# A router and two feed-forward layers on one core: token rows gathered in quarters and transposed on VectorE

## The chip, the cores and the metric

The kernel runs on one core of a Trainium2 chip. The metric is the device time of one execution in microseconds (us), the median of three runs. Engines are named as the profile names them: PE is TensorE's matmul, PEld its weight load, DVE is VectorE, ACT is ScalarE, POOL is GpSimd, and SP is SyncE, which issues most transfers.

## The reference

```python
B, H, S, D = 4, 12, 448, 64          # attention; N = B*S = 1792 tokens of H*D = 768
scores = q @ k.T / sqrt(D) - log(S)
attn_out = sigmoid(scores) @ v       # -> x[1792, 768]

logits = x @ w_gate                  # 8 experts, each takes cap = 224 tokens:
# the pairs (token, expert) are walked in falling order of logit; a token goes to the
# first expert that still has room
for e in range(8):
    out[mask_e] = relu(x[mask_e] @ w1[e]) @ w2[e]      # 768 -> 1024 -> 768

h = out @ w_in                       # 768 -> 2048
return (s * relu(h)**2 + b) @ w_out  # 2048 -> 768
```

Everything is float32. The kernel keeps that precision by splitting each operand into a high part (`float32r`) and a low part, the remainder, and summing three products: high by high, high by low and low by high.

## The kernel before, in words

The order of the work is written out by hand (`manual_schedule`): each engine executes its instructions in the order in which the program names them, and semaphores are put in where data are shared.

**Attention and routing.** The first part computes attention, writes the token rows to a scratch tensor `xs` in DRAM, and decides by an auction which 224 tokens go to which expert. `places` leaves the token numbers in `idx`, a tile of 128 partitions by 2 halves by 8 experts: column e of half h holds the rows of expert e, 128 in the first half and 96 in the second. `keep_clock` puts matmuls on zeros into PE's queue while PE has nothing else to do. `gather(0)` then fetches the rows of expert 0, and a branch (`go_on`) on a flag skips the fallback of the auction.

**Four groups.** The rest is a loop over g = 0..3. Each group has three stages:

- *Experts*: `expert(2g)` and `expert(2g+1)`, each with 8 weight units of the first layer (`w1`, 6 blocks of 128x128) and 6 of the second (`w2`, 8 blocks). `half_mm` does a unit with two matmuls per block, 448 columns (high and low of the data side by side) and 224 columns; the last two units of `w1` use `short_mm`. After each unit, ACT and DVE make the high and low parts of the result.
- *Hidden*: 16 units (`f` in `range(KG)`), each of 18 matmuls of 448 columns, then square, scale and shift on ACT and DVE.
- *Output*: two halves `h`, 8 units (`span`) each, with three tiles of 128 rows in even groups and four in odd groups, 6 matmuls of 384 columns per tile and unit. The results go to `orow` and are written to the output by `scatter` on POOL's queue, later, in the next even expert.

**Weights.** All units stand in one list. `advance`, called once per unit, issues the load of a unit up to 8 ahead (`w_dma`, on SP), makes the low part of a unit 4 ahead (`w_low`) and the high part of one 5 ahead (`w_high`, on ACT). There are 4 raw buffers and 5 each for high and low, so a load waits until the low part of the unit four places in front has been made. The list `where` says which low parts POOL makes; the others are DVE's:

```python
where += [n in (0, 2, 4, 6, 12) for n in range(KF + KD)]   # L171, for every expert
```

**Rows of an expert.** `gather(e)` issues two indirect DMAs on POOL's queue, 128 and 96 rows of 3 KB. `x_split(e, n)`, n = 0..3, transposes three 128-column blocks of one half on PE (L653) into PSUM; ACT copies the high part to `xg[e]` (L655) and DVE subtracts to make the low part (L656). An even expert's four pieces are put into the hidden stage of the group in front (L778, at f = 3, 7, 11, 15), an odd expert's into the even expert in front of it (L710, at f = 1 to 4). `gather(2g+2)` is issued behind `expert(2g)` (L757), `gather(2g+3)` behind the hidden stage (L782).

**Other work in these stages.** `row_ids` (16 small copies on POOL, L632) makes the lists for `scatter`; it stands behind `gather(1)`, in front of the first expert (L751). In group 0, `late_convert` (four DVE instructions, L151 to L154, each time on a 768 KB load into one buffer) brings the last 8 blocks of 64-bit weights to float32: five times in the hidden stage, three times in the output stage (h = 0, units 0, 2 and 4).

Of the kernel before, what the change touches and what calls it, by code (L numbers as in the profile page):

```python
# [8 lines left out]
F32 = mybir.dt.float32  # L9
F32R = mybir.dt.float32r  # L10
BF16 = mybir.dt.bfloat16
I32 = mybir.dt.int32
# [18 lines left out]
KG = F2 // 128  # L31
HT = (128, CAP - 128)
DH = DM // 2
LEVELS = 8
GROW = 2.0
MARGIN = 0.25
# [20 lines left out]
C_FLAT = C_F + LEVELS + 2  # L57
C_SEL = C_FLAT + CP
C_OFF = C_SEL + E
C_END = C_OFF + LEVELS + 2  # L60


@with_exitstack
def tile_kernel(ctx, tc, qT, kT, v, wg, w1, w2, wi, wo, s2, b2, cst, out):
# [4 lines left out]
    wraw = ctx.enter_context(tc.tile_pool(name="wraw", bufs=4))  # L69
    wsp = ctx.enter_context(tc.tile_pool(name="wsp", bufs=5))  # L70
    wlp = ctx.enter_context(tc.tile_pool(name="wlp", bufs=5))
    xrp = ctx.enter_context(tc.tile_pool(name="xrp", bufs=2))
    dpool = ctx.enter_context(tc.tile_pool(name="dpool", bufs=1, space=DRAM))
    ctx.enter_context(tc.manual_schedule())

# [3 lines left out]
    sb2 = const.tile([128, 2], F32, name="sb2")  # L79
    idx = const.tile([128, 2, E], I32, name="idx")  # L80
    idt = const.tile([128, 3, 4], I32, name="idt")
    idl = const.tile([128, 2], I32, name="idl")
    spacer = const.tile([1, 1], F32, name="spacer")

# [82 lines left out]
    for g in range(4):  # L167
        for e in (2 * g, 2 * g + 1):
            units += [(w1[e, f], KD, True) for f in range(KF)]
            units += [(w2[e, d], KF, True) for d in range(KD)]  # L170
            where += [n in (0, 2, 4, 6, 12) for n in range(KF + KD)]  # L171
        units += [(narrow[i], wide[i][1], False) for i in range(len(wide))]
        where += [False] * len(wide)
    raws, splits = {}, {}
# [188 lines left out]
    for n, c in ((0, C_ID), (2, C_SAMEE), (3, C_PREV), (4, C_TRI), (5, C_NEGE)):  # L363
        G.tensor_copy(cb[:, n], ct[:, c:c + 128])
    V.scalar_tensor_tensor(cb[:, 1], ct[:, C_ID:C_ID + 128], -2.0, ct[:, C_SAMEC:C_SAMEC + 128],
                           op0=ALU.mult, op1=ALU.add)
    G.tensor_copy(off, ct[:2, C_OFF:C_END])
    G.memset(two, 1.0)
    G.tensor_copy(slot, ct[:, C_SLOT:C_SLOT + CAP])
    identb, rival, samee, prev, tri, nege = (cb[:, n] for n in range(6))  # L370
# [145 lines left out]
    oh = rp.tile([CP, NCH, CAP], BF16, name="oh")  # L516
    ia = rp.tile([128, 2, E], F32, name="ia")
    Pf = P.rearrange("p c e -> p (c e)")

    def places(rest=lambda: None):  # L520
        pp = ps_1.tile([CP, 128], F32, name="pa")
        T.matmul(pp, ch, identb, start=True, stop=True)
        V.tensor_copy(cw, cnt0.to_broadcast([128, CP]))
        po = ps_r.tile([CP, NCH, E], F32, name="pi")
        pof = po.rearrange("p c e -> p (c e)")
        T.matmul(pof, cw, prev, start=True, stop=False)
        V.tensor_copy(Pf, pp)
        T.matmul(pof, tri[:CP, :CP], Pf, start=False, stop=True)
        V.tensor_mul(pm_, po, P)
        V.reduce_sum(pos, pm_, axis=AX.X)  # L530
        for c in range(NCH):
            V.tensor_scalar(oh[:, c], slot[:CP], pos[:, c:c + 1], None, op0=ALU.is_equal)
            if c == 2:
                pk = count()
            if c == 5:
                full(pk)
                rest()
            if c == 3:
                G.tensor_mul(R[:, :, 0, :], P, ct[:CP, C_CIDX:C_CIDX + 128].rearrange("p (c e) -> p c e", e=E))
                A.mul(R[:, :, 1, :], P, ct[:CP, C_P:C_P + 1])  # L540
        pis = [ps_r.tile([n, 2, E], F32, name="pi") for n in HT]
        for c in range(NCH):
            for h, n in enumerate(HT):
                T.matmul(pis[h].rearrange("p a e -> p (a e)"), oh[:, c, h * 128:h * 128 + n],
                         R[:, c].rearrange("p a e -> p (a e)"), start=(c == 0), stop=(c == NCH - 1))
        for h, n in enumerate(HT):
            A.copy(ia[:n, h], pis[h][:, 1])
            V.scalar_tensor_tensor(idx[:n, h], pis[h][:, 0], float(CP), ia[:n, h], op0=ALU.mult, op1=ALU.add)

    xr = {}  # L550

    def gather(e):
        if e >= E:
            return
        for h, n in enumerate(HT):
            if (e, h) not in xr:
                xr[e, h] = xrp.tile([128, DM], F32, name="xr")
            G.indirect_dma_start(out=xr[e, h][:n], out_offset=None, in_=xs,
                                 in_offset=bass.IndirectOffsetOnAxis(ap=idx[:n, h, e:e + 1], axis=0))

    auction(STEPS, True)
    places(lambda: rows(len(turns)))
# [42 lines left out]
    def go_on(steps):  # L605
        rv = nc.values_load(flag[0:1, 0:1], min_val=0, max_val=128)
        with tc.If(rv < 128):
            if steps:
                auction(steps[0], False)
                full(count())  # L610
                go_on(steps[1:])
            else:
                greedy()
            if steps == MORE:
                places()
                gather(0)

    gather(0)
    go_on(MORE)
    rt.close()  # L620
    early.close()
# [22 lines left out]
    def x_split(e, n):  # L644
        if e >= E:
            return
        if n == 0:
            xg[e] = m2p.tile([128, KD, 2, CAP], F32R, name="x")
        h, k0 = n // 2, n % 2 * 3
        m = HT[h]  # L650
        px = ps_x.tile([128, 3, 128], F32, name="px") if e else ps_m.tile([128, 3, 128], F32, name="acc")
        for k in range(3):
            T.transpose(px[:, k, :m], xr[e, h][:m, (k0 + k) * 128:(k0 + k + 1) * 128], ident[:m, :m])  # L653
        xh = xg[e][:, k0:k0 + 3, 0, h * 128:h * 128 + m]
        A.copy(xh, px[:, :, :m])  # L655
        V.tensor_sub(xg[e][:, k0:k0 + 3, 1, h * 128:h * 128 + m], px[:, :, :m], xh.bitcast(F32))  # L656
# [38 lines left out]
    def expert(e, y):  # L695
        x = xg.pop(e)
        u = ml.tile([128, KF, 2, CAP], F32R, name="u")
        for f in range(KF):
# [7 lines left out]
                if f == KF - 2:  # L706
                    advance()
            if 1 <= f <= 4:
                if e % 2 == 0:
                    x_split(e + 1, f - 1)  # L710
                if out_rows:
                    scatter(*out_rows.pop(0))
        sl = slice((e % 2) * CAP, (e % 2 + 1) * CAP)
        for d in range(KD):
            wh, wl = w_get()
            half_mm(wh, wl, u, KF, AF.Copy, (y[:, d, 0, sl], y[:, d, 1, sl]), d < KD - 1)

    def scatter(ids, row):
        G.memset(spacer, 0.0)
# [24 lines left out]
        last["i"] += 1  # L744
        late_in()

    stores, out_rows = [], []
    for n in (0, 2, 1, 3):
        x_split(0, n)
    gather(1)  # L750
    row_ids()  # L751
    last["buf"] = ml.tile([128, 3072], I32, name="orow")
    late_in()
    for g in range(4):
# [8 lines left out]
        for f in range(KG):  # L763
# [9 lines left out]
            else:  # L773
                A.activation(gn[:, f, 0], r, AF.Identity, bias=sb2[:, 1:2])  # L774
            V.scalar_tensor_tensor(gn[:, f, 1], r, sb2[:, 1:2], gn[:, f, 0].bitcast(F32),
                                   op0=ALU.add, op1=ALU.subtract)
            if f % 4 == 3:
                x_split(2 * g + 2, f // 4)  # L778
            advance()
            if not g and f % 3 == 1:  # L780
                late_convert()
        gather(2 * g + 3)  # L782
        tiles = [(128 * t, idt[:, t - 1, g:g + 1]) for t in range(1, 4)]
        if g % 2:
            tiles = [(0, idl[:, g // 2:g // 2 + 1])] + tiles
# [2 lines left out]
        for h in range(2):  # L788
# [3 lines left out]
            for span in spans:  # L792
                ws = {u: [w.rearrange("p k c -> p (k c)") for w in w_get()] for u in span}
                for t, (c0, ids) in enumerate(tiles):
# [8 lines left out]
                    if span[-1] == n - 1:  # L803
# [8 lines left out]
                            scatter(ids, orow[:, t])  # L812
                        elif h:
                            out_rows.append((ids, orow[:, t]))
                advance()
                if not g and not h and span in ([0], [2], [4]):
                    late_convert()
# [2 lines left out]
def _consts(np):  # L820
# [17 lines left out]
    c[1, C_OFF] = 0.0  # L838
    c[:2, C_OFF + LEVELS + 2 - SIGNS:C_OFF + LEVELS + 2] = np.float32([[NT - CAP], [0.5]])
    c[:, C_FLAT:C_FLAT + CP] = FLATC - ((CP * ch[:, None] + np.arange(CP)[None]) * E + e[:, None])  # L840
    c[:, C_SEL:C_SEL + E] = (p[:, None] % 32) == np.arange(E)[None]
    return c


def _layout(np, i):
    c = np.ascontiguousarray

    def heads(a):
# [4 lines left out]
        "kT": c(heads(i["k"]).transpose(0, 1, 2, 4, 3).reshape(B, NP, 128, S)),  # L853
        "v": c(i["v"].reshape(B, NP, 2, NC, CP, D).transpose(0, 1, 4, 3, 2, 5).reshape(B, NP, CP, NC, 128)),
        "wg": c(i["moe_w_gate"].reshape(KD, 128, E).transpose(1, 0, 2)),
        "w1": c(i["moe_w1"].reshape(E, KD, 128, KF, 128).transpose(0, 3, 2, 1, 4)),
        "w2": c(i["moe_w2"].reshape(E, KF, 128, KD, 128).transpose(0, 3, 2, 1, 4)),
        "wi": c(i["moe2_w_in"].reshape(KD, 128, KG, 128).transpose(2, 1, 0, 3)).view(np.int64),
        "wo": c(i["moe2_w_out"].reshape(8, 2, 128, 2, DH).transpose(3, 0, 2, 1, 4)
# [22 lines left out]
```

## Time and profile before

| | before |
|---|---|
| three runs | 944.69 us median (944.27 to 946.06) |
| profiled execution | 946.52 us, span 944.7 us |
| PE busy | 917.0 us, 97% of the span |
| PEld, DVE, ACT, POOL busy | 84%, 62%, 48%, 15% |
| mean granted TensorE clock | 0.983 |

The span runs from the first to the last instruction; 1.8 us of the profiled time lie around it. The profiled execution was 1.83 us above the median of the three runs. Busy time is what the engines' records cover; matmuls are pipelined, so that a matmul's own duration is longer than the step from one to the next. "Idle before" in a timeline names what ended the wait.

### The profile page before, as it was taken

To read this page: it belongs to the slowest core of one execution; us is meant where nothing else is said; L and a number is where in the kernel's file an instruction comes from. 1 tells how busy PE (TensorE), PEld (TensorE's weight loads), DVE (VectorE), ACT (ScalarE), POOL (GpSimd) and SP (SyncE) were. 2 spreads that over 40 slices of the span, in tenths; PEclk is the share of its full clock that TensorE was granted. 3 is DMA by queue.
4 is the path that set the end of the run, shared out by engine and by line. 5 is a ranking of instruction groups with operands and counts; after the bars stand their busy time and mean duration, and the time that the engine had idled before them with its cause. 6 is when DMAs were issued, how large, how long until landed. Compare 5 with 4: busy or idle time off the path is not lost.

```text
span 944.7 us, 14521 instructions
## 1 busy us (share of the span) xinstructions
PE 917.0 (97%) x5467; PEld 797.0 (84%) x5467; DVE 587.6 (62%) x1043; ACT 449.3 (48%) x787; POOL 138.1 (15%) x136
## 2 busy tenths in 40 slices
PE   9999999688999999999999999999999999999997
PEld 4454555568999999999999999999999999999997
DVE  3877875645868875578776224786773287777320
ACT  6666767735654432566333225564332366433120
POOL 1000003224410000442000004420000232100001
PEclk9999999779999999999999999999999999999999
DMA  9989993844746666567334235763444476433311
GB/s 307 321 298 341 321 323 111 241 134 167 239 144 214 219 230 217 179 222 230 119 117 141 90 101 165 232 218 122 129 127 137 119 251 211 137 120 108 126 34 68
DMA packets 68459, 173.12 MB, mean 183 GB/s; under 512 B 7968, under 2 KB 24864, under 8 KB 68384
## 3 DMA queue, kind: packets, MB, share of 16 engines
q1 hardware_dynamic: 66112, 161.13, 52.9%
q0 software_dynamic: 2272, 11.01, 3.4%
q8 instruction: 44, 0.72, 0.3%
q14 instruction: 31, 0.25, 0.1%
HBM read 148.52 MB, written 23.59 MB: 182 GB/s over the span
## 4 chain that ended last, share of the span: by engine, by line
PE 56%; DVE 10%; DMA 5%; ACT 3%; issue 2%; POOL 1%; POOLq 0%; SPq 0%; ACTq 0%; DVEq 0%
PE acc L661 9%; PE acc L801 7%; PE acc L802 7%; PE acc L800 7%; PE acc L727 6%; PE acc L728 6%; PE acc L729 6%; PE acc L662 4%; DVE wl L201 4%; DMA raw<-in_w_dram 3%; DMA orow<-in_wo_dram 2%; ACT wh L190 1%; DVE y L675 1%; ACT gt L774 1%; DVE r L770 1%
## 5 line engine op out<-in xcount | busy, mean ns | idle before, releaser
L190 ACT CAST wh<-raw 128x768 fp32r<-128x768 f32 (+1 forms) x240 | 208.8, 877 | 160.6 <-PE acc L802 115.7
L201 DVE TENSOR_TENSOR wl<-raw,wh 128x768 fp32r<-128x768 f32 (+1 forms) x198 | 207.2, 1053 | 91.1 <-ACT wh L190 91.1
L201 POOL TENSOR_TENSOR wl<-raw,wh 128x768 fp32r<-128x768 f32 (+1 forms) x42 | 92.6, 2213 | 414.8 <-ACT wh L190 414.7
L801 PE MATMUL acc<-wl,gt 128*128 128x384 f32 x448 | 150.4, 336 | 1.8 <-DVE wl L201 1.8
L800 PE MATMUL acc<-wh,gt 128*128 128x384 f32 x448 | 150.6, 336 | 0.0
L802 PE MATMUL acc<-wh,gt 128*128 128x384 f32 x448 | 150.4, 336 | 0.0
L727 PE MATMUL acc<-y,wh 128*128 128x448 f32 x384 | 141.4, 368 | 0.0
L729 PE MATMUL acc<-y,wl 128*128 128x448 f32 x384 | 140.6, 366 | 0.0
L728 PE MATMUL acc<-y,wh 128*128 128x448 f32 x384 | 140.6, 366 | 0.0
L661 PE MATMUL acc<-u,wh 128*128 128x448 f32 x384 | 121.9, 376 | 1.8 <-DVE u L685 1.5
L662 PE MATMUL acc<-u,wl 128*128 128x224 f32 x384 | 101.4, 264 | 0.0
L661 PE MATMUL acc<-x,wh 128*128 128x448 f32 x288 | 94.4, 383 | 0.7 <-DVE x L656 0.7
L251 ACT ACTIVATE attn<-psc,nls 112x896 f32<-112x896 f32 x96 | 88.8, 1008 | 9.4 <-PE psc L249 9.4
L769 ACT ACTIVATE r<-acc 128x448 f32<-128x448 f32 x64 | 34.8, 543 | 116.7 <-PE acc L729 116.7
L801 PEld LDWEIGHTS acc<-wl,gt 128*128 128x128 f32 x448 | 84.7, 189 | 2.1 <-DVE wl L201 2.1
L800 PEld LDWEIGHTS acc<-wh,gt 128*128 128x128 f32 x448 | 84.7, 189 | 0.0
L802 PEld LDWEIGHTS acc<-wh,gt 128*128 128x128 f32 x448 | 84.5, 189 | 0.0
L662 PE MATMUL acc<-x,wl 128*128 128x224 f32 x288 | 76.8, 267 | 3.0 <-POOL wl L201 3.0
L661 PEld LDWEIGHTS acc<-u,wh 128*128 128x128 f32 x384 | 72.1, 188 | 8.9 <-DVE u L685 3.6
L260 PE MATMUL pv<-attn,vt 112*64 112x448 f32 x384 | 77.5, 545 | 0.0
L729 PEld LDWEIGHTS acc<-y,wl 128*128 128x128 f32 x384 | 72.1, 188 | 6.3
L728 PEld LDWEIGHTS acc<-y,wh 128*128 128x128 f32 x384 | 72.2, 188 | 6.1
(212 smaller groups left out, 1306.7 us busy)
## 6 DMA issues: line engine op xcount, KB each, us to landing
raw<-nw SPq DMA_DIRECT2D x128, 384.0 KB, 3.0
raw<-in_w_dram SPq DMA_DIRECT2D x64, 384.0 KB, 3.9
raw<-in_w_dram SPq DMA_DIRECT2D x48, 512.0 KB, 4.5
craw<-in_wi_dram SPq DMA_DIRECT2D x16, 768.0 KB, 5.8
nw<-co SPq DMA_DIRECT2D x24, 384.0 KB, 7.7
craw<-in_wo_dram SPq DMA_DIRECT2D x8, 768.0 KB, 6.3
orow<-in_wo_dram SPq DMA_DIRECT2D x8, 768.0 KB
rqk<-in_kT_dram SPq DMA_DIRECT2D x24, 224.0 KB, 6.9
```

Of the source, the lines that this page charges most:

```text
L190: A.copy(h[:, :k], raws[i][:, :k])
L201: eng.tensor_sub(lo[:, :k], r[:, :k], h[:, :k].bitcast(F32))
L251: A.activation(attn[n][:, :, c, :], p[:, :, :S], AF.Sigmoid, bias=nls[:CP], scale=1.0 / math.sqrt(D))
L260: T.matmul(pv[j * 64:(j + 1) * 64, :S], v[:, c, j * D:(j + 1) * D], a[:, j, c, :], start=(c == 0), stop=(c == NC - 1))
L661: T.matmul(p[:, :2 * CAP], wh[:, k], src[:, k].rearrange("p a s -> p (a s)"), start=(k == 0), stop=False)
L662: T.matmul(p[:, :CAP], wl[:, k], src[:, k, 0], start=False, stop=(k == n - 1))
L727: T.matmul(p, wh, src[:, k, 0], start=first, stop=False)
L728: T.matmul(p, wh, src[:, k, 1], start=False, stop=False)
L729: T.matmul(p, wl, src[:, k, 0], start=False, stop=last)
L800: T.matmul(ps[t][:, :DH], hi, wh[:, cols], start=(f == 0), stop=False)
L801: T.matmul(ps[t][:, :DH], hi, wl[:, cols], start=False, stop=False)
L802: T.matmul(ps[t][:, :DH], lo, wh[:, cols], start=False, stop=(f == KG - 1))
```

## The change

From expert 2 on, a gather fetches quarter rows: `xs` is seen as 7168 rows of 192 columns, and each of seven indirect DMAs brings 32 tokens, of each the four quarters to four groups of 32 partitions. With 32 tokens by 192 columns on each group of 32 partitions, a transpose of 32 by 32 blocks on DVE gives the layout that the matmuls need, with the contracted dimension in another order; the rows of `w1` for experts 2 to 7 are put into the same order on the host. `x_split` for these experts moves to the output stage of the group in front (units 1 to 4 of each half), and its subtraction to the unit behind. `gather(2g+3)` follows the even expert's last transpose there. The index list `idq` for the quarters is made by `spread`, behind `gather(0)`, with seven small matmuls. Besides this, `row_ids` moves into expert 0's second layer, and POOL makes the low parts of units 6 and 12 alone for experts 1 to 7.

```diff
-    xrp = ctx.enter_context(tc.tile_pool(name="xrp", bufs=2))
+    xrp = ctx.enter_context(tc.tile_pool(name="xrp", bufs=1))
...
-            where += [n in (0, 2, 4, 6, 12) for n in range(KF + KD)]
+            where += [n in ((0, 2, 4, 6, 12) if e else (6, 12)) for n in range(KF + KD)]
...
@@ places, at c == 3
                 A.mul(R[:, :, 1, :], P, ct[:CP, C_P:C_P + 1])
+                A.copy(pick, ident.rearrange("p (j r) -> p j r", r=32)[:, :, None, :].to_broadcast([128, 4, 4, 32]))
...
+    def spread():
+        for h, n in enumerate(HT):
+            V.tensor_copy(idf[:n, h], idx[:n, h])
+        pq = ps_r.tile([128, NJ, E], F32, name="pi")
+        for j in range(NJ):
+            n = HT[j // 4]
+            T.matmul(pq[:, j], pick[:n, j % 4].rearrange("p q r -> p (q r)"), idf[:n, j // 4], start=True, stop=True)
+        V.tensor_scalar(idq, pq, 4.0, ct[:, C_QUAD:C_QUAD + 1], op0=ALU.mult, op1=ALU.add)
+
     def gather(e):
         if e >= E:
             return
-        for h, n in enumerate(HT):
-            if (e, h) not in xr:
-                xr[e, h] = xrp.tile([128, DM], F32, name="xr")
-            G.indirect_dma_start(out=xr[e, h][:n], out_offset=None, in_=xs,
-                                 in_offset=bass.IndirectOffsetOnAxis(ap=idx[:n, h, e:e + 1], axis=0))
+        if e not in xr:
+            xr[e] = xrp.tile([128, 2 * DM], F32, name="xr")
+        if e < 2:
+            for h, n in enumerate(HT):
+                G.indirect_dma_start(out=xr[e][:n, h * DM:(h + 1) * DM], out_offset=None, in_=xs,
+                                     in_offset=bass.IndirectOffsetOnAxis(ap=idx[:n, h, e:e + 1], axis=0))
+        else:
+            for j in range(NJ):
+                G.indirect_dma_start(out=xr[e][:, j * DQ:(j + 1) * DQ], out_offset=None,
+                                     in_=xs.rearrange("t (q d) -> (t q) d", q=4),
+                                     in_offset=bass.IndirectOffsetOnAxis(ap=idq[:, j, e:e + 1], axis=0))
...
     gather(0)
+    spread()
     go_on(MORE)
...
@@ x_split
+        if e > 1:
+            j0, nj = 2 * n, min(2, NJ - 2 * n)
+            px = ps_x.tile([128, 2 * DQ], F32, name="px")[:, :nj * DQ]
+            V.transpose(px, xr[e][:, j0 * DQ:(j0 + nj) * DQ])
+            px = px.rearrange("p (j k r) -> p k j r", j=nj, r=32)
+            hi, lo = (xg[e][:, :, a, j0 * 32:(j0 + nj) * 32].rearrange("p k (j r) -> p k j r", r=32) for a in range(2))
+            A.copy(hi, px)
+            rest.append((lo, px, hi))
+            return
...
@@ expert
             if 1 <= f <= 4:
-                if e % 2 == 0:
-                    x_split(e + 1, f - 1)
+                if not e:
+                    x_split(1, f - 1)
...
             half_mm(wh, wl, u, KF, AF.Copy, (y[:, d, 0, sl], y[:, d, 1, sl]), d < KD - 1)
+            if not e and d == 1:
+                row_ids()
...
     gather(1)
-    row_ids()
...
@@ hidden stage
-            if f % 4 == 3:
-                x_split(2 * g + 2, f // 4)
             advance()
             if not g and f % 3 == 1:
                 late_convert()
-        gather(2 * g + 3)
...
@@ output stage, after the matmuls of a unit
+                for lo, px, hi in rest:
+                    V.tensor_sub(lo, px, hi.bitcast(F32))
+                rest.clear()
+                if g < 3 and 1 <= span[0] <= 4:
+                    x_split(2 * g + 2 + h, span[0] - 1)
+                    if not h and span[0] == 4:
+                        gather(2 * g + 3)
                 advance()
```

`spread` also stands in the fallback of the auction, behind its `gather(0)`. The constants get one more column, `C_QUAD` (p // 32).

## Rows read from the trace of the kernel before

**Rows 1.** The page, part 1: busy us (share of the span) and instructions.

```profile
PE 917.0 (97%) x5467; PEld 797.0 (84%) x5467; DVE 587.6 (62%) x1043; ACT 449.3 (48%) x787; POOL 138.1 (15%) x136
```

**Rows 2.** Windows by stage: length, PE, PEld, DVE, ACT, POOL busy, clock, DMA, GB/s.

```profile
207.06:243.95 36.89, 33.91 (x217) 31.83 (x217) 23.11 (x37) 20.17 (x42) 16.97 (x24) 0.95 0.55 182
243.95:274.82 30.87, 30.58 (x206) 29.13 (x205) 24.07 (x38) 20.05 (x41) 8.28 (x5) 1.00 0.72 228
...
334.89:388.53 53.64, 51.89 (x291) 51.57 (x290) 28.15 (x37) 16.83 (x23) 4.79 (x3) 0.97 0.64 212
388.53:420.05 31.52, 31.52 (x218) 30.32 (x217) 25.24 (x37) 20.41 (x42) 15.28 (x12) 1.00 0.70 224
...
609.41:641.27 31.86, 30.87 (x206) 29.15 (x205) 24.25 (x38) 20.15 (x41) 8.89 (x5) 1.00 0.70 222
641.27:701.33 60.06, 60.06 (x302) 55.04 (x301) 43.44 (x67) 21.52 (x36) 0.98 (x1) 1.00 0.37 113
701.33:751.34 50.01, 50.01 (x291) 50.01 (x290) 16.82 (x21) 15.07 (x20) 4.59 (x3) 1.00 0.46 140
...
813.67:872.05 58.38, 58.38 (x290) 54.12 (x289) 42.04 (x63) 20.45 (x33) 0.00 (x0) 1.00 0.36 109
```

**Rows 3.** Timeline of POOL in expert 0: start, us, instruction [idle before].

```profile
207.61 0.92 POOL L558 DMA_INDIRECT xr<-xs,idx  x1 [0.30 <-issue]
212.00 3.68 POOL L632 COPY idt<-idx 32x4 int32<-32x4 int32 x12 [3.48 <-DMA xr<-xs,idx]
...
216.64 4.26 POOL L201 TENSOR_TENSOR wl<-raw,wh 128x768 fp32r<-128x768 f32 x2
```

**Rows 4.** Timeline of PE in expert 0, fifth weight unit.

```profile
219.17 0.37 PE L662 MATMUL acc<-x,wl 128*128 128x224 f32 x1 [2.96 <-POOL wl L201]
```

**Rows 5.** Window of four us behind that wait, columns as in group 2.

```profile
219.00:223.00 4.00, 3.83 (x16) 3.60 (x17) 0.00 (x0) 0.30 (x1) 1.90 (x2) 0.59 0.72 240
```

**Rows 6.** Timeline of PE in expert 2, around one group of three transposes.

```profile
392.18 0.27 PE L662 MATMUL acc<-x,wl 128*128 128x224 f32 x1
392.28 0.49 PE L653 MATMUL px<-ident,xr 128*128 128x128 f32 x3
...
392.81 0.26 PE L662 MATMUL acc<-x,wl 128*128 128x224 f32 x1
...
393.12 0.27 PE L662 MATMUL acc<-x,wl 128*128 128x224 f32 x1
```

**Rows 7.** Line L653, the transposes: ns min/median/max, first and last start.

```profile
L653 PE MATMUL px<-ident,xr x84: 243/270/367, 211.1 to 761.8; 128*128 128x128 f32 x42, 96*128 96x96 f32 x42
```

**Rows 8.** Timeline of POOL and DVE in expert 4.

```profile
582.65 2.11 POOL L201 TENSOR_TENSOR wl<-raw,wh 128x768 fp32r<-128x768 f32 x1 [0.41 <-ACT wh L190]
...
582.97 2.04 DVE L672 SCALAR_TENSOR_TENSOR u<-tt,u 128x224 fp32r<-128x224 f32 x1
```

**Rows 9.** Lines L201 (low part of a weight) and L672, as group 7.

```profile
L201 DVE TENSOR_TENSOR wl<-raw,wh x198: 941/952/2581, 212.0 to 918.9; 128x768 fp32r<-128x768 f32 x158, 128x1024 fp32r<-128x1024 f32 x40
...
L672 DVE SCALAR_TENSOR_TENSOR u<-tt,u x48: 378/393/2040, 211.4 to 797.4; 128x224 fp32r<-128x224 f32 x48
```

**Rows 10.** Tile xr: the gathers on POOL's queue, and issue to landing.

```profile
L558 POOL DMA_INDIRECT xr<-xs,idx x16: 914/968/1180, 198.7 to 701.8; - x16
...
DMA to landing us min/median/max: 4.0/4.6/6.1
```

**Rows 11.** Line L656, the low part of the rows, as group 7.

```profile
L656 DVE TENSOR_TENSOR x<-px,x x28: 449/498/557, 213.2 to 764.5; 128x384 fp32r<-128x384 f32 x14, 128x288 fp32r<-128x288 f32 x14
```

**Rows 12.** Timeline of DVE in group 0's output stage.

```profile
361.33 0.56 DVE L151 TENSOR_SCALAR orow<-orow 128x768 int32<-128x768 int32 x1 [4.19 <-DMA orow<-in_wo_dram]
...
364.14 1.82 DVE L201 TENSOR_TENSOR wl<-raw,wh 128x768 fp32r<-128x768 f32 x2
```

**Rows 13.** Timeline of PE at the same place.

```profile
365.15 0.44 PE L801 MATMUL acc<-wl,gt 128*128 128x384 f32 x1 [1.75 <-DVE wl L201]
```

**Rows 14.** Groups by line: busy us, mean ns of one, idle before.

```profile
L287 PE MATMUL small<-ct,lg 128*112 128x8 f32 x32 | 3.8, 245 | 0.0
```

More of the change, by code (lines that the diff above doesn't have):

```diff
@@ L33 @@
 DH = DM // 2
+NJ = CAP // 32
+DQ = DM // 4
 LEVELS = 8
@@ L59 @@
 C_OFF = C_SEL + E
-C_END = C_OFF + LEVELS + 2
+C_QUAD = C_OFF + LEVELS + 2
+C_END = C_QUAD + 1
 @with_exitstack
@@ L81, in tile_kernel @@
     idt = const.tile([128, 3, 4], I32, name="idt")
+    idq = const.tile([128, NJ, E], I32, name="idq")
     idl = const.tile([128, 2], I32, name="idl")
@@ L366, in tile_kernel @@
                            op0=ALU.mult, op1=ALU.add)
-    G.tensor_copy(off, ct[:2, C_OFF:C_END])
+    G.tensor_copy(off, ct[:2, C_OFF:C_QUAD])
     G.memset(two, 1.0)
@@ L518, in tile_kernel @@
     Pf = P.rearrange("p c e -> p (c e)")
+    idf = rp.tile([128, 2, E], F32, name="idf")
+    pick = rp.tile([128, 4, 4, 32], F32, name="pick")
     def places(rest=lambda: None):
@@ L616, in go_on @@
                 gather(0)
+                spread()
     gather(0)
+    spread()
     go_on(MORE)
@@ L652, in x_split @@
         for k in range(3):
-            T.transpose(px[:, k, :m], xr[e, h][:m, (k0 + k) * 128:(k0 + k + 1) * 128], ident[:m, :m])
+            c0 = h * DM + (k0 + k) * 128
+            T.transpose(px[:, k, :m], xr[e][:m, c0:c0 + 128], ident[:m, :m])
         xh = xg[e][:, k0:k0 + 3, 0, h * 128:h * 128 + m]
@@ L745, in late_convert @@
         late_in()
-    stores, out_rows = [], []
+    stores, out_rows, rest = [], [], []
     for n in (0, 2, 1, 3):
@@ L840, in _consts @@
     c[:, C_FLAT:C_FLAT + CP] = FLATC - ((CP * ch[:, None] + np.arange(CP)[None]) * E + e[:, None])
+    c[:, C_QUAD] = p // 32
     c[:, C_SEL:C_SEL + E] = (p[:, None] % 32) == np.arange(E)[None]
@@ L855, in _layout @@
         "wg": c(i["moe_w_gate"].reshape(KD, 128, E).transpose(1, 0, 2)),
-        "w1": c(i["moe_w1"].reshape(E, KD, 128, KF, 128).transpose(0, 3, 2, 1, 4)),
+        "w1": c(np.concatenate([
+            i["moe_w1"][:2].reshape(2, KD, 128, KF, 128).transpose(0, 3, 2, 1, 4),
+            i["moe_w1"][2:].reshape(E - 2, 4, KD, 32, KF, 128).transpose(0, 4, 1, 3, 2, 5)
+            .reshape(E - 2, KF, 128, KD, 128)])),
         "w2": c(i["moe_w2"].reshape(E, KF, 128, KD, 128).transpose(0, 3, 2, 1, 4)),
```

## The prediction

> **What bounds the kernel now.** I read the page first: PE has work on it for 97% of the span [rows 1], so the time is what PE executes, plus what it waits, plus what it loses to a lower clock. Then the stretches, one for each stage from expert 0 on [rows 2]. Two comparisons matter. The hidden stage of group 2, with four groups of transposes in it, takes 60.06 us (group 0's 60.07 and group 1's 60.06 are like it); that of group 3, with the same matmuls and no transposes, 58.38. And expert 0 takes 36.89 where expert 2, with the same units and transposes, takes 31.52 (expert 6 the same). In no stage from expert 0 on is DVE busy for more than four fifths of the time. Last I looked at what PE waits for. From expert 0 on there are only a few such places: 2.96 us for a low part made by POOL in expert 0 [rows 4], 1.75 us for one made by DVE in group 0's output stage [rows 13], and short ones where the second layer of an expert starts.
>
> **The change part by part.**
>
> *Transposes leave PE.* 72 of the 96 go (experts 2 to 7). A transpose is recorded with a median of 270 ns [rows 7], but that is latency: around a group of three, the step from one matmul on line 662 to the next is 0.63 us where the next plain step is 0.31 [rows 6], so that three transposes cost 0.32 us. In a hidden stage the whole saving is 60.06 - 58.38 = 1.68 us [rows 2], three times: -5.0. In experts 2, 4 and 6 it is four groups of 0.32, a little less for the two groups with 96 rows: 1.2 us, three times: -3.6. Bounds: 6 x 1.2 = 7.2 and 6 x 1.68 = 10.1. Sum of the two: -8.6.
>
> The Trainium skill ("TensorE: Matmul & The Clock Gate", Part 4: PE-mode transpose) gives about 275 ns for a transpose in a kernel's context, which this trace's 270 ns matches. Taken as PE's time it would make 72 x 0.275 = 19.8 us, an estimate by that page, and a total 11 us lower than mine; the steps in the timeline are what speaks against it.
>
> *The row lists leave the front of expert 0.* POOL issues the gather of expert 1, waits 3.48 us, makes the 16 small copies and comes to its first low part at 216.64 [rows 3]. PE needs that one and waits 2.96 us [rows 4]; behind the wait, the granted clock over four us is 0.59, part of that time being at 1.2 GHz instead of 2.4 [rows 5], which costs another 4.0 x 0.41 = 1.6. After the change POOL can begin when the gather is issued (208.5), or, if it still waits for the landing, at 212.0; with 2.1 us for the unit it is done by 214.2, two us before PE needs it. Gain 4.6 by these rows; by the comparison of experts 0 and 2 it is 5.4, but that holds the filling of the first units too. I take -4.7, bounds 3.0 (only the wait) and 5.4. In their new place the copies stand on POOL behind expert 0's last low part, and the next user of the lists is in expert 2, so they cost nothing there; with less room they would hold the gather of expert 2 for 4.5 us, which has two stages of time.
>
> *Low parts go from POOL to DVE* (21 units). This is not simply more work for DVE. While POOL makes a low part (582.65 to 584.76), a DVE instruction that began beside it takes 2.04 us [rows 8] where its median is 0.393 [rows 9]: POOL's unit costs DVE 1.6 us, DVE's own takes 0.95 [rows 9]. So DVE gets some 0.7 us back per unit. In even experts the four subtractions of `x_split`, 0.5 us each, go as well. A DVE unit of the first layer then needs 0.38 + 0.39 + 0.95 = 1.7 us against PE's 6 x 0.31 = 1.9: it fits, with little to spare. What expert 5 (31.86) and its like lose today is measured against 84 steps of 0.31 us [rows 6] and 36 short matmuls, each a little over a third of a step, an estimate of 30.4: 0.5 for expert 1 (30.87), 1.5 for expert 5 [rows 2], about 0.4 each for experts 3, 7 and 4, which repeat expert 1's pattern: 3.1 in all. I take 1.0 of it back; bounds: all of it, or 4.5 lost where the gathers' small transfers get in the way of the weights in experts 1, 3 and 5.
>
> *Gathers.* Seven per expert instead of two. An issue takes POOL 0.97 us [rows 10] and the next follows 0.30 later [rows 3], so seven take 8.9 us, and the last has landed 4.6 us after its issue [rows 10]: some 13.5 us. For odd experts they start behind the transpose of unit 4 of h = 0, and the first reader is five units on, 5 x 3.1 us = 15.6 (output stages of 50.01 us have 16 units). Two us of margin, and behind it the low parts are four units ahead, 12.5 us. Even experts' rows come a whole stage early. POOL has nothing else to do there. Cost: nothing, as long as that holds.
>
> *The transposes on DVE.* No such instruction is in the trace. The nearest row is the subtraction from PSUM, 498 ns for 384 or 288 columns [rows 11]; I take 0.5 us for the transpose. The lower bound is the same work at no cost, the upper one 2.0 us, the longest that an instruction of that size shows here [rows 9]. In the output stages DVE is busy a third of the time (16.82 of 50.01 us) [rows 2], so that in groups 1 and 2 even 2 us per unit fits into 3.1. The place where it may not is group 0: there DVE waits for the loads of `late_convert`, 4.19 us each time [rows 12], and then has to catch up on low parts; PE waits 1.75 us [rows 13], and with the slow clock behind it the stage is 53.64 - 50.01 = 3.6 us longer than group 2's [rows 2]. The new work between two conversions (two transposes, two subtractions, 2.0 us) fits into the 4.19 us of waiting. One subtraction comes behind the last conversion, directly in front of the low part that PE wants: +0.5. The gather of expert 3 now runs beside the last of these loads: some tenths more. On the other side the three subtractions that leave the hidden stage let the conversions start 1.3 us sooner, but PE arrives 1.7 us sooner as well. I take +0.8, bounds 0 and +4.
>
> *`spread`.* Its seven matmuls stand behind the keep-warm matmuls and in front of the branch, in the shortest gap of the kernel. The nearest row, float32 with 8 columns, is 3.8 us for 32, 0.12 each [rows 14]: +0.8, and the chain through DVE a tenth more: +0.9. Bounds 0 (the rows of expert 0 land later anyway) and 7 x 0.245 = 1.7. The copy that makes `pick` is covered by ACT's idle time in front of `idx`; without that cover it would cost what a copy of 512 columns costs, some 0.6 us.
>
> *Sum:* -8.6 - 4.7 - 1.0 + 0.8 + 0.9 = -12.6. Against the profiled execution, 946.52, that is 933.9; this one was 1.83 above the median of the runs. Against the median, 944.69: **932.1 us**.
>
> **Rivals.**
> 1. *The quarter rows crowd the weights.* DMA is busy for 70% in the experts [rows 2], and pieces of 768 bytes take more of it than rows of 3 KB. Then experts 1, 3 and 5 each lose another 1.5 us, as expert 5 does now, instead of getting 1.0 back in all: 932.1 + 1.0 + 4.5 = 937.6. Against it: the bytes are the same, and POOL's slow low parts no longer hold the loads back.
> 2. *The transpose on DVE is slow.* Up to 1.5 us it fits group 0's wait. At 2.5 us, the last two gaps run over by 1 to 2 us each, PE waits that and runs slowly behind it: about +6, 938.
> 3. *The gathers land one after another.* Seven at 4.6 us are 32 us where 15.6 are to be had. DVE stands in front of its first transpose for 17 us, the lead of 12.5 is used up, and PE waits 4 us or more in groups 0 and 2, twice that with the clock as it fell behind the other waits: +17, that is 949, slower than before. It decides from about 28 us on. Against it: the second gather is issued 0.30 us behind the first and not behind its landing [rows 3]. The rule that speaks for it is in the Trainium skill ("DMA: Bandwidth & Descriptors", Bandwidth and Anatomy of one DMA): small transfers are mostly fixed cost, about 2 us each plus the bytes. By its formula seven in a row are an estimate of 15.6 us, no later than the reader, so that by the page alone nothing is lost.
> 4. *Everything that experts lose at the start of the second layer goes*, with group 0's stage unchanged and `spread` hidden: 932.1 - 2.1 - 0.8 - 0.9 = 928.3.
> 5. *Moving the row lists does nothing*, since POOL is late for another reason: 936.8.
>
> **How the numbers follow.** Forecast 0.70; rival 1: 0.10; 2: 0.06; 3: 0.04; 4: 0.08; 5: 0.02. The forecast's own range is 929.5 to 935.5. With rivals 1 and 4 the range is 928.0 to 937.7, which leaves out rival 3, most of 2 and the outer ends of the forecast. What can be told from no change here is about 0.2%, 1.9 us. Faster by more than that: the forecast, 1, 4, 5 and most of 2, less what the bounds together may bring, 0.93; slower is rival 3, 0.04; within 0.2%, 0.03.
>
> **What would show it.** Right: hidden stages of groups 0 to 2 at 58.4 us; expert 0 near 32, with no PE wait for POOL and a clock of 1.00 behind its start; experts 2, 4 and 6 near 30.5; DVE's 0.39 us instructions no longer at 2 us from expert 1 on but for two units each; DVE transposes near 0.5 us; group 0's output stage still near 54 us. Wrong: a wait of PE for a low part in the output stages of groups 1 and 2 (rival 3), a first unit of the second layer that starts 1.5 us late in experts 1, 3 and 5 (rival 1), or a DVE transpose of over 1.5 us (rival 2).

## Result: slower by 1.1%, and the profile after

The changed kernel takes 956.25 us (median of 4 runs, 954.66 to 958.60), the kernel before on the same chip 945.38 (944.27 to 948.49): ratio 1.0113, 95% interval 1.0091 to 1.0134. The prediction was 932.1 in a range of 928.0 to 937.7, with 0.04 on slower. It was wrong, by 24 us and in sign.

One mistake has to be put right before anything else is read. The new `where` line is `(0, 2, 4, 6, 12) if e else (6, 12)`. It cuts POOL's low parts for **expert 0 alone**; experts 1 to 7 keep all five. The section on the change and the prediction say the opposite. What goes to DVE is three units, not 21, and POOL's queue keeps its low parts in just those experts where the new gathers are issued.

The profiled run (956.43 us, span 954.6) by stage, windows of the changed kernel with the columns of [rows 2]; in order: experts 0 and 1, group 0's hidden and output stage, experts 2 and 3, and (behind the dots) expert 5:

```profile
213.80:246.95 33.15, 32.56 (x218) 30.75 (x217) 22.74 (x38) 19.80 (x42) 14.28 (x22) 0.99 0.52 168
246.95:283.55 36.60, 32.33 (x206) 30.44 (x205) 24.45 (x38) 20.56 (x42) 14.94 (x11) 0.95 0.69 224
283.55:341.93 58.38, 58.38 (x291) 54.12 (x290) 43.58 (x63) 27.90 (x46) 0.00 (x0) 1.00 0.56 183
341.93:393.68 51.75, 50.53 (x289) 49.88 (x288) 34.85 (x53) 19.14 (x30) 11.36 (x9) 1.00 0.68 227
393.68:424.17 30.49, 30.49 (x206) 29.14 (x205) 23.63 (x33) 19.09 (x38) 15.22 (x12) 1.00 0.72 232
424.17:460.88 36.71, 32.72 (x207) 30.55 (x205) 23.77 (x38) 20.07 (x41) 13.05 (x10) 0.95 0.61 192
...
618.01:652.26 34.25, 31.05 (x206) 29.14 (x205) 22.50 (x38) 20.15 (x41) 12.93 (x10) 1.00 0.65 205
```

Beside [rows 2] the account of the 9.9 us between the spans (944.7 and 954.6) closes. Lost: 6.7 in front of expert 0 (first matmul of its first unit at 213.80, before at 207.06), 5.7 in expert 1, 6.1 in expert 3, 2.4 in expert 5, 0.2 in expert 4, 1.65 behind the last matmul. Gained: 3.7 in expert 0, 3 x 1.68 in the hidden stages, 1.9 in group 0's output stage, 1.0 and 0.8 in experts 2 and 6, 0.3 in others.

What PE waits for from expert 0 on, in the changed kernel, the four largest (us in total, times, longest):

```profile
PE acc L696 <- POOL wl L205: 8.5, 3, 3.7
PE acc L687 <- DVEq L629: 4.2, 1, 4.2
PE acc L695 <- DVE u L719: 4.1, 5, 1.6
PE acc L833 <- DVE wl L205: 1.2, 2, 1.0
```

**Loss 1: a queue on POOL.** The units of an expert are counted from 0 here: 0 to 7 are its first layer, 8 to 13 its second. POOL's timeline in expert 3 (start, us, instruction, idle time before):

```profile
421.15 2.24 POOL L205 TENSOR_TENSOR wl<-raw,wh 128x768 fp32r<-128x768 f32 x1 [3.15 <-ACT wh L194]
423.55 0.98 POOL L579 DMA_INDIRECT xr<-xs,idq  x1 [0.16 <-issue]
...
431.71 0.95 POOL L579 DMA_INDIRECT xr<-xs,idq  x1 [0.30 <-issue]
432.68 3.61 POOL L205 TENSOR_TENSOR wl<-raw,wh 128x768 fp32r<-128x768 f32 x2
```

and PE's:

```profile
434.54 0.38 PE L696 MATMUL acc<-x,wl 128*128 128x224 f32 x1 [2.48 <-POOL wl L205]
```

Seven issues hold POOL from 423.55 to 432.66, 9.1 us, and the low parts of expert 3's units 4 and 6 stand behind them (unit 2's is the one at 421.15, in front of them; the expectation of e1 below names the units wrongly). Unit 4 takes 4.63 us where 1.88 is plain, that is, without a wait; in experts 1 and 5 it is 7.27 and 4.49. Those three make 10.75 of the 14.2 us that experts 1, 3 and 5 lose: 8.5 us of waiting, as listed above, and slower matmuls behind the longest wait (granted clock 0.50, that is 1.2 of 2.4 GHz, from 259.38 to 262.00). Most of the rest is the start of expert 3's second layer (units 8 and 9, 4.53 and 4.10, before 2.88 and 2.51).

**Loss 2: `spread` stands in front of a branch.** PE and DVE before expert 0, then DVE's part of the branch's line in both kernels (name, count, duration in ns, first and last start):

```profile
205.51 1.62 PE L565 MATMUL pi<-idf,pick 128*128 128x8 f32 x14
211.35 2.47 PE L687 MATMUL acc<-ident,xr 128*128 128x128 f32 x12 [4.22 <-DVEq L629]
```

```profile
207.18 0.28 DVE L566 TENSOR_SCALAR idq<-pi,ct 128x56 int32<-128x56 f32 x1 [7.63 <-PE pi L565]
212.82 0.92 DVE L690 TENSOR_TENSOR x<-acc,x 128x384 fp32r<-128x384 f32 x2 [5.37 <-ACT x L689]
```

```profile
L629 DVEq EVENT_SEMAPHORE  x2: 21/21/21, 211.1 to 211.2; - x2
L629 DVEq COMPARE_BRANCH  x1: 72/72/72, 208.2 to 208.2; - x1
```

```profile
L607 DVEq EVENT_SEMAPHORE  x2: 21/21/21, 204.1 to 204.2; - x2
L607 DVEq COMPARE_BRANCH  x1: 72/72/72, 199.7 to 199.7; - x1
```

The last fence is the kernel before: DVE came to the branch at 199.7 and was through at 204.1, while PE did its keep-warm matmuls. In the changed kernel DVE's last instruction of `spread` waits for matmuls behind those, so DVE comes to the branch at 208.2, is through at 211.1, and PE stands still for 4.22 us. For the next 2.45 us PE's granted clock is 0.50, where the kernel before has 1.00 at this place.

What went as forecast: the hidden stages at 58.38; the transposes on DVE; and no wait for rows in an output stage (the transposes' line, the first here, lists none in front of it; the second is the line of the new gathers):

```profile
L676 DVE STREAM_TRANSPOSE px<-xr x24: 364/582/587, 353.5 to 747.4; 128x384 f32<-128x384 f32 x18, 128x192 f32<-128x192 f32 x6
```

```profile
L579 POOL DMA_INDIRECT xr<-xs,idq x42: 945/952/1635, 248.5 to 732.6; - x42
```

### The profile page after: what moved, and what is told of

Its sections match the earlier page's. It is cut to its first block, busy times and chain, and to the rows that moved or that the text cites. A ratio compares the mean times of both kernels' runs of the same rounds, so it can differ in the third digit from the quotient of the medians.

```text
span 954.6 us, 14507 instructions
## 1 busy us (share of the span) xinstructions
PE 915.6 (96%) x5409; PEld 795.0 (83%) x5409; DVE 596.4 (62%) x1071; ACT 450.2 (47%) x788; POOL 167.4 (18%) x165
## 4 chain that ended last, share of the span: by engine, by line
PE 44%; issue 16%; DVE 8%; DMA 4%; ACT 2%; POOL 2%; SPq 0%; POOLq 0%; DVEq 0%; ACTq 0%
PE acc L695 10%; PE acc L696 5%; PE acc L833 5%; PE acc L834 5%; PE acc L832 5%; PE acc L763 4%; PE acc L765 4%; PE acc L764 4%; DVE wl L205 3%; DMA raw<-in_w_dram 3%; DMA orow<-in_wo_dram 1%; POOL xr L579 1%; ACT gt L809 1%; DVE r L805 1%; POOL wl L205 1%
## 5 line engine op out<-in xcount | busy, mean ns | idle before, releaser
L205 POOL TENSOR_TENSOR wl<-raw,wh 128x768 fp32r<-128x768 f32 (+1 forms) x41 | 87.7, 2148 | 329.8 <-ACT wh L194 322.0
L579 POOL DMA_INDIRECT xr<-xs,idq x42 | 45.3, 1079 | 264.0 <-DVE px L676 252.6
```

Of the source, the lines that this page charges most:

```text
L205: eng.tensor_sub(lo[:, :k], r[:, :k], h[:, :k].bitcast(F32))
```

## Experiments

### e1_low_parts_dve: low parts of the odd experts off POOL

```diff
-            where += [n in ((0, 2, 4, 6, 12) if e else (6, 12)) for n in range(KF + KD)]
+            where += [n in (6, 12) for n in range(KF + KD)]
```

> The changed kernel, but POOL makes only the low parts of units 6 and 12 in every expert; DVE takes units 0, 2 and 4. Queue theory: in experts 1, 3 and 5, POOL's low parts of units 2 and 4 stand behind seven gathers (8.9 us) in POOL's queue and PE waits for them. Then these three experts fall from 36.6, 36.7 and 34.3 us to about 30.7, and the time from 956.3 to about 941, before's or a little under it. Transfer theory (rival): the quarter rows crowd the weight loads; then the three experts stay above 33 us and the time above 949. A third possibility, that DVE cannot carry three more low parts, would show as longer experts 2, 4, 6 and 7 (30.5 to 32.2 now): each 1 us or more longer.

Measured: 943.32 us (10 runs), ratio to before 0.9997 (0.9974 to 1.0019), span 940.1. Its PE waits:

```profile
PE acc L687 <- DVEq L629: 4.2, 1, 4.2
PE acc L695 <- DVE u L719: 2.6, 4, 1.1
```

No wait for POOL is left, unit 4 is at 1.88 in every odd expert, and 13 us of the loss are gone. The gathers are issued at the same places as with the change, so it was not their transfers that cost the time. But for the three units of expert 0, this is the kernel that the prediction was made for, and it takes 943.3, not 932.1: the misread line is not the only mistake. The wait behind the branch is untouched.

### e2_gather_late: the gathers moved behind the low parts instead

```diff
         expert(2 * g, y)
-        gather(2 * g + 2)
         expert(2 * g + 1, y)
+        gather(2 * g + 2)
```

> The changed kernel, but the gather of experts 2, 4 and 6 is issued behind the odd expert instead of in front of it; POOL keeps its low parts. Queue theory: experts 1, 3 and 5 go back to what they were before the change (30.9, 30.7, 31.9), the time to about 942. If only the number of DVE's or POOL's low parts mattered, they would stay above 33 us. The rows then come in the hidden stage, which has 58 us before the first transpose, so nothing new is waited for.

Measured: 945.17 us, ratio 1.0004 (0.9984 to 1.0025). PE waits for POOL nowhere, with all five low parts left on POOL. Both ways of separating the seven issues from the low parts work: it is their order in one queue that costs. The 942 that was expected is missed by 3 us: expert 1 still takes 33.4 us (before 30.9), with two short waits for low parts made by DVE and a late unit 8 (3.98 us).

### e3_spread_late: `spread` behind the branch

```diff
     gather(0)
-    spread()
     go_on(MORE)
...
             if not e and d == 1:
                 row_ids()
+                spread()
```

> The changed kernel, but the index list for the quarters is made inside expert 0, behind the row lists, instead of in front of the branch. Branch theory: the DVE instruction that ends the list stands in front of DVE's branch, the branch takes DVE 3 to 4 us, and PE waits for DVE behind it (4.2 us); moved, expert 0 starts at about 208 us instead of 213.8, with the seven matmuls costing expert 0 up to 0.9 us: 951 us. Rival: what delays expert 0 is PE's own 1.6 us of matmuls there; then it starts at 212 and the time is 954 to 955.

Measured: 955.15 us, ratio 1.0106 (1.0076 to 1.0136). Expert 0 does start at 206.89, 6.9 us sooner than with the change, so loss 2 is `spread` in front of the branch. But the gain is lost again in the new place:

```profile
233.58 3.13 PE L567 MATMUL px<-idf,pick 128*128 128x8 f32 x14 [3.92 <-DVE idf L563]
```

So 951 us is missed by 4. PE waits 3.92 us for the index copies, which DVE gets to late, and behind that wait the matmuls run 3.13 us, at a granted clock of 0.50 (1.62 in the changed kernel, at 1.00); units 9 and 10 of expert 0 take 9.56 and 4.05 us.

### e4_spread_early: keep-warm matmuls behind `spread`'s

```diff
-    keep_clock(WARM[1], ...)
...
     gather(0)
     spread()
+    keep_clock(WARM[1], ...)
     go_on(MORE)
```

> The changed kernel, but the keep-warm matmuls are put behind the seven matmuls of the index list instead of in front of them, so that DVE ends the list some 5 us sooner and goes into its branch sooner. Branch theory: DVE is through its branch at 205 to 206.5 instead of 211.1 us, expert 0 starts at 207.5 to 209 and the time is 951 to 952. Rival (PE's own matmuls): the same matmuls are still in front of expert 0, the gain is at most what PE waits less, under 1 us.

Measured: 953.90 us, ratio 1.0098 (1.0062 to 1.0134). DVE is through the branch 4.3 us sooner and PE's wait for it is gone, but PE's own stream now ends at 209.5; expert 0 starts at 212.19, 1.6 sooner than with the change. The matmuls (2.98 us here, in front of the keep-warm matmuls and at a granted clock of 0.50, where behind those they take 1.62 at 1.00) and what they wait for on DVE (0.67) take PE's time wherever they stand in front of expert 0.

### f1_both and f2_both_gather_late: both losses repaired

`spread` behind the branch with its index copies already at unit 4 of expert 0, and low parts as in e1; f2 has the gathers of e2 besides.

```diff
+            if not e and f == 4:
+                spread_ids()
...
             if not e and d == 1:
                 row_ids()
+                spread()
```

> The changed kernel with both mends: POOL makes only the low parts of units 6 and 12 in every expert, and the index list for the quarters is made inside expert 0, its two DVE copies at unit 4 of the first layer, so that its matmuls in the second layer do not wait for them. If the two causes are separate and are all of the loss, the gains add: 943.3 (with the first mend alone) minus the 6.9 us by which expert 0 started sooner with the list moved, plus up to 1.6 us for the matmuls: 936.5 to 938, under the kernel before. If DVE is what limits the experts now, their second layers start late and the time stays near 942.

> The kernel of the run before, and the gather of experts 2, 4 and 6 behind the odd expert. If the quarter rows crowd the weight loads in experts 1, 3 and 5, their late starts of the second layer (1.6, 0.2 and 0.4 us with POOL's low parts moved) go, and the time is 1 to 2 us below the run before. If they do not, it is the same within 1 us.

Measured: f1 940.31 us, ratio 0.9957 (0.9935 to 0.9978); f2 938.97, ratio 0.9943 (0.9924 to 0.9963). Faster than before, and the wait at `spread` is gone (expert 0's units 9 and 10: 3.99 and 2.59, its matmuls alone). But f1 is 2.3 us above the upper end of what was expected, with late starts of the second layer that come to 8.2 us in its profiled execution (unit 8, over 2.51 us in each expert) where e1's come to 4.5; and f2 is 1.3 us below f1, which lies within the spread of either, so that it doesn't settle whether the gathers crowd the weights there. What is left in f2:

```profile
PE acc L697 <- DVE u L721: 5.0, 7, 1.3
```

### e7_front_of_expert0 and e8_lists_alone: the row lists by themselves

Kernel before, with `row_ids` in expert 0's second layer (e8), and with expert 0's low parts cut too (e7).

```diff
     gather(1)
-    row_ids()
...
+            if not e and d == 1:
+                row_ids()
```

> The kernel before with two parts of the change alone: the row lists moved into expert 0's second layer, and POOL making only units 6 and 12 in expert 0. The 3.0 us wait for POOL and the slow clock behind it in expert 0 go: 944.9 - 4.7 = 940.2. If something else takes their place, 943 or more.

> The kernel before with the row lists moved alone; POOL keeps units 0, 2, 4, 6 and 12 in expert 0. If the lists in front of POOL's first low part were the cause of the wait, as predicted, this is as good as the run before it: 940. If the number of low parts on POOL was, the wait stays: 944.

Both missed: e7 946.94 us, ratio 1.0016 (0.9994 to 1.0037); e8 946.12, ratio 1.0004 (0.9985 to 1.0023). In e8, expert 0 did become 4.7 us shorter (32.2), and expert 1 5.3 longer (36.2). (e8's profiled execution took 951.01 us, 4.9 above its median; expert 7's second layer alone loses 3.7 us at its start there, so its stages are read here and not its total.) Its POOL shows where the copies went:

```profile
228.70 2.79 POOL L201 TENSOR_TENSOR wl<-raw,wh 128x1024 fp32r<-128x1024 f32 x1 [14.15 <-ACT wh L190]
231.56 3.99 POOL L632 COPY idt<-idx 32x4 int32<-32x4 int32 x12
235.59 1.68 POOL L632 COPY idl<-idx 32x2 int32<-32x2 int32 x4
237.35 3.67 POOL L201 TENSOR_TENSOR wl<-raw,wh 128x768 fp32r<-128x768 f32 x2
```

Behind expert 0's last low part and the copies stand expert 1's first two low parts, made four units ahead. The raw buffer that such a low part reads comes free late, the load into it starts late (at 239.23, and takes 5.25 us), and ACT and PE come to a stop:

```profile
244.56 0.83 ACT L190 CAST wh<-raw 128x768 fp32r<-128x768 f32 x1 [6.85 <-DMA raw<-in_w_dram]
...
248.45 0.56 PE L662 MATMUL acc<-x,wl 128*128 128x224 f32 x1 [2.54 <-DVE wl L201]
```

### g1_lists_hidden: the row lists where POOL has nothing to do

```diff
             if not g and f % 3 == 1:
                 late_convert()
+            if not g and f == 2:
+                row_ids()
```

in the hidden stage of group 0, otherwise as e7.

> The kernel before, with expert 0's low parts on POOL cut to units 6 and 12 and the sixteen small copies of the row lists moved out of the experts altogether, to the third unit of group 0's hidden stage. In the two kernels that put these copies into expert 0's second layer, expert 0 became 4.3 to 4.7 us shorter and expert 1 3.0 to 5.3 us longer: POOL made the copies for 5.7 us in front of the low parts of expert 1's first units, and a weight buffer whose last reader is such a low part was loaded late (ACT waited 6.85 us for a load). Theory A (POOL's queue): with the copies out of the way expert 0 and expert 1 together take 67.8 - 4.4 = 63.4 us or a little less, and the kernel 940.3. Theory B (the weights' loads can't come faster than they did, whatever stands on POOL): expert 1 stays 3 us longer than before, the two take 66 to 67 us, and the kernel 945 to 946.

Measured: 940.90 us (9 runs), ratio 0.9950 (0.9928 to 0.9971). Experts 0 and 1 together take 63.31, before 67.76, and e7's 66.48. The 4.7 us were real; the new place was the fault.

### g2_lists_hidden_f2: the same in f2

> The best kernel so far (the change with low parts 6 and 12 alone on POOL for every expert, the index arithmetic inside expert 0, the even experts' gather behind the odd expert: 938.97) with the row lists' copies moved to group 0's hidden stage. There POOL has no low part of expert 1's first layer to make, so that the copies held nobody: by theory A (only a queue with low parts behind the copies costs) no change, 939; if the copies' time on POOL costs DVE through slower instructions beside them, expert 0's units 9 and 10 (3.99 and 2.59 us where 2.51 is plain) come back by some tenths, 938.5.

Measured: 938.33 us, ratio 0.9927 (0.9899 to 0.9954), by medians as good as f2. Units 9 and 10 of expert 0 stay at 3.99 and 2.58, so the copies had not held anybody there.

### g4_advance_late: what makes the second layer start late

```diff
             else:
                 short_mm(wh, wl, x, KD, (u[:, f, 0], u[:, f, 1]))
-                if f == KF - 2:
+                if f == KF - 1:
                     advance()
```

on top of g2.

> As the kernel with row lists in the hidden stage, and the weight work that stands between the two short units at the end of an expert's first layer (issue of loads, one low part, one cast) moved behind the second of them. In the trace of the combined kernel ACT's cast there waits up to 2.19 us for its weight load, the activation of the last unit of the first layer stands behind it in ACT's queue, and PE waits for that activation: unit 8 of experts 1 to 7 takes 2.95 to 4.1 us instead of 2.51, about 7 us in all with the slow clock. Theory A (order in ACT's queue): the activation no longer waits, unit 8 is back at 2.51 in most experts, and 5 to 7 us are gained: 932 to 934. Theory B (the loads are too late in any case): the wait moves to a unit one or two further on, for the cast or its low part, and the time stays within 2 us of the kernel without the edit.

Measured: **933.04 us** (932.07 to 934.05, 6 runs), ratio 0.9862 (0.9836 to 0.9889), the best kernel here. In g2, a cast waited for its weight load, and the activation that PE needs stood behind it in ACT's queue:

```profile
586.99 1.05 ACT L197 CAST wh<-raw 128x1024 fp32r<-128x1024 f32 x1 [3.20 <-DMA raw<-in_w_dram]
587.94 0.35 ACT L720 ACTIVATE u<-acc 128x224 fp32r<-128x224 f32 x1
```

```profile
588.77 0.47 PE L697 MATMUL acc<-u,wh 128*128 128x448 f32 x1 [1.25 <-DVE u L721]
```

In g4 the activation goes first, at the same place and in every expert:

```profile
584.10 0.36 ACT L720 ACTIVATE u<-acc 128x224 fp32r<-128x224 f32 x1 [0.65 <-PE acc L718]
585.27 2.22 ACT L197 CAST wh<-raw 128x1024 fp32r<-128x1024 f32 x2 [0.81 <-DMA raw<-in_w_dram]
```

Unit 8 is at 2.50 to 2.51 us in all eight experts, and PE's waits for `u` are gone. The loads are no earlier: ACT still waits for them, and longer in sum than in f2. ACT's waits between 199 and 860 us (us in total, times, longest), in f2 and then in g4:

```profile
ACT wh L197 <- DMA raw<-in_w_dram: 19.5, 17, 3.1
```

```profile
ACT wh L197 <- DMA raw<-in_w_dram: 26.6, 32, 1.9
```

In g2, from which g4 is made, that sum is 18.0 us. Now nothing that PE needs soon is queued behind these waits. The edit moves three things at once, the issue of loads, a low part and a cast; that it is the cast is read from the timeline and not tried by itself.

### g5_repairs_without_change: what the change itself is worth

g1 with the edit of g4: transposes on PE, whole rows, no `spread`.

> The kernel before with the three repairs that don't need the change: row lists in the hidden stage, expert 0's low parts on POOL cut to units 6 and 12, and the weight work between the two short units moved behind the second. Transposes stay on TensorE, gathers are whole rows. It tells what the change itself is worth beside the best kernel (933.0). By the first reckoning, the terms of the prediction: the transposes on PE cost 8.6 (hidden stages 5.0, experts 2, 4 and 6 3.6), the index arithmetic inside expert 0 costs the best kernel 1.6, group 0's output stage is 2 to 3 us shorter in the best kernel: 942 to 943, no better than the kernel with the lists moved (940.9). By the second, from that kernel's own medians and the late starts of its second layers in the trace (unit 8: 0.35, 0.23, 0.93, 0.23 and 1.95 us, 3.7 in all): 937. The two differ in whether the late starts were really worth 3.7 us where the transposes remain, so the start of the second layer decides: if unit 8 of every expert is at 2.51 and the time is 937, the change is worth 4 us of the 12 gained; if 942, nearly 10.

Measured: 939.33 us (8 runs), ratio 0.9937 (0.9915 to 0.9959), between the two reckonings. Unit 8 is at 2.51 everywhere, as the second said; by medians that gave 1.6 us over g1 and not 3.7. Against g5, g4 is 6.3 us faster (933.04 and 939.33); the two ran on different chips, and by their ratios to the kernel before, 0.9862 and 0.9937, it is 7.1. Stage by stage in the two profiled runs: hidden stages 3 x -1.68; experts 2+3, 4+5 and 6+7 -1.20, -1.19 and -1.04 (61.86 each in g5); start of expert 0 +1.0 (0.7 of it there already where the routing ends); `spread` in experts 0 and 1 +1.6; group 0's output stage +0.3; the end +1.3: 4.4 between the spans 935.5 and 931.1. g5's profiled execution took 937.25 us, 2.1 under its median, and g4's 933.13, 0.1 over: that is how 4.4 and 6.3 stand to each other.

## Why the prediction was wrong, step by step

*Transposes leave PE, -8.6: right.* Hidden stages -1.69, -1.69, -1.68 in the changed kernel; an even expert's four groups gave 1.20, 1.19 and 1.04 (g5 against g4), forecast 1.2: -8.5. The reading of steps in the timeline instead of recorded durations held. The Trainium skill's figure ("TensorE: Matmul & The Clock Gate", Part 4: PE-mode transpose, about 275 ns), taken as PE's time, would have made an estimated 19.8; the runs do not agree with that use of it.

*Gathers, 0: the step that failed first.* "POOL has nothing else to do there" is false. The sentence rested on the misread `where` line. With the line read rightly, the working of the prediction gives the loss: 8.9 us of issues stand in front of the low part of a unit that is made four units, 7.5 us, ahead. Listing POOL's queue, in order, in the even and in the odd expert would have caught it. What the prediction did argue about gathers, their landing and the crowding of DMA (rivals 1 and 3), was no trouble: no transpose waited for rows, and the DMA share in experts 2 and 3 is 0.72 and 0.61, before up to 0.72. A late unit 8 in an odd expert, rival 1's sign, did show (expert 1 in e1: 4.15 us), but in f2 as well, where the gathers come behind the odd expert (3.85). Rival 3 was on the right side of no change for a wrong reason.

*`spread`, +0.9, bounds 0 and 1.7: the step that failed next.* Expert 0 starts 6.7 us later. 0.9 of that is there already where the routing ends and is not `spread`'s price: DVE's last instruction of the routing starts at 199.11 us here and at 198.25 before, but at 198.54 in e2, which has the change's front, and at 199.31 in g1, which has nothing of it. The matmuls took 1.6 and not 0.8: the 32 of [rows 14] are two records for each of 16 float32 matmuls in the program, as the seven of `spread` are 14 records, so that 0.12 us was the price of half a matmul. PE's wait behind the branch became 4.2 where it was 0.6; the rest is PE's slower work around it. I priced the matmuls and the chain through DVE, and did not ask what stands behind DVE's last instruction. That is the branch, whose 4.4 us in the kernel before were hidden beside the keep-warm matmuls. The cover was moved away: DVE now comes to the branch 8.5 us later, and PE's keep-warm matmuls are done by then.

*Row lists, -4.7: size right, place wrong.* Expert 0 gained 3.7 in the changed kernel, 4.7 in e8 and 4.3 in g1. But "the copies stand on POOL behind expert 0's last low part ... so they cost nothing there" left out that low parts run four units ahead, so that expert 1's stand behind the copies. In e8 that took all of the 4.7, in e7 3.0 of 4.3, and e7's medians show nothing of the rest; in g1, with the lists in the hidden stage, 4.45 of it stayed. Rival 5's result, nothing gained, came in e7 and e8, and its cause, that POOL was late for another reason, did not. In the changed kernel expert 0 kept its 3.7; the copies there stand in front of expert 1's low parts and the seven issues, and of the three waits for POOL expert 1's is the longest (3.7 us). How much of that is the copies' was not tried.

*Low parts to DVE, for the late starts of the second layer, -1.0: wrong mechanism.* They were put down to POOL's slow low parts and to DVE. e1 takes 24 units from POOL that the kernel before leaves there, and unit 8 is no better (in all 4.5 us over eight plain units of 2.51, before 3.5). What stood there was a cast that waits for a load, in front of an activation in ACT's queue (g4).

*Group 0's output stage, +0.8: it became 1.9 us shorter* (51.75 against 53.64), with PE waiting 0.19 and 1.03 us for low parts where [rows 13] has 1.75. The stage is not only the change's: e7, with none of the new work in it, has 51.20, g5 51.58, e8 54.06 and g1 54.59; the nine kernels with the change all have 51.3 to 52.0. What decides between the two values was not tried.

*The transpose on DVE, 0.5 us: 0.58.* Rival 2 fell.

So the forecast's own sum, 932.1, and the best kernel's 933.0 are close, but not for the forecast's reasons; that it comes out is luck. g4 pays 1.6 us for `spread` (0.9 in the sum) and 1.3 at the end (nothing in the sum), and has its late starts repaired by an edit that the change doesn't contain.

## What to carry to other kernels

Write out each engine's queue around every instruction that is added or moved, with the work that runs ahead for the next stage in it, and ask of each item behind it who waits; three of the five wrong terms here were such an item (low parts behind gathers, low parts behind copies, an activation behind a cast), the fourth was a branch that lost its cover, and the fifth, group 0's output stage, is not explained. Read a condition in a diff by evaluating it for two values before building on it. When an edit gains what was forecast in its stage and the total doesn't move, look one stage further before calling the gain false.

## What was not expected of the hardware

At the branch, DVE needs 4.4 us from its compare to the event that follows in the kernel before, and 2.9 in the changed one; ACT needs 0.5 there (199.8 to 200.3 in the changed kernel). The four kernels with `spread` in front of the branch have 2.8 to 2.9 for DVE, the ten others 4.0 to 4.4. Why they differ was not tried.

Behind the last transfer's issue POOL's longest drain takes 4.53 us in the kernel before and 6.19 in the changed one:

```profile
L878 POOLq DRAIN  x3: 46/112/4529, 939.4 to 944.5; - x3
```

```profile
L921 POOLq DRAIN  x3: 46/113/6193, 947.6 to 954.4; - x3
```

It is 4.52 to 4.54 in e7, e8, g1 and g5, which gather whole rows, and 6.18 to 6.19 in all the others (e1 to e4, f1, f2, g2, g4), which issue 42 gathers of quarter rows. That is the 1.65 us behind the last matmul. The number of issues from POOL (16 gathers before, 46 after) goes with it; whether it is the number or the kind was not tried.
